# w3 times w_out as three fp32r products, w1 and w2 decoded once, landmark matrices evicted from a pair of PSUM banks

## The chip, the cores and the metric

One NeuronCore of a Trainium2 chip runs the whole program. The metric is the device time of one execution in microseconds (us). PE is the matmul engine, DVE, ACT and POOL are the vector, scalar and GpSimd engines, SP is the queue from which nearly all transfers are issued.

## The reference

Three layers follow each other, all to be computed to fp32 accuracy (fp32r is the one-pass matmul type, whose operands have fewer bits; a number is then carried as a high and a low half):

```python
# 4 batches, 8 heads, 576 tokens, 64 per head, 32 landmarks of 18 tokens
A = sm(q, k_lm); Bm = sm(q_lm, k_lm); C = sm(q_lm, k)      # scaled softmaxes
Z = Bm.transpose(0, 1, 3, 2) / (norm_1(Bm) * norm_inf(Bm) + 1e-06)
for _ in range(6):
    Z = 2 * Z - Z @ Bm @ Z
x = A @ Z @ C @ v                                          # 2304 x 512
h = (x @ w1) * (x @ w2) @ w3 @ w_out                       # w3 1024x1024, w_out 1024x512
h = h @ w_in; g = h * tanh(softplus(h)); out = g @ w_out2  # 512x2048, 2048x512
```

The weights come as float64.

## The kernel before

`ORDER` is one long string of step names, written out by hand; `issue()` walks through it and emits every step on its engine (the step's first engine, or the one behind `@`). Each engine executes its own instructions in that order. A step takes tiles from named pools (`take`) and gives them back (`free`), so the string also decides who waits for whose buffer. The last 14 of 24 output groups stand in an ordinary loop behind it.

**Weights.** A piece is 128 rows by 512 float64. `ld` (SP) loads it into a slot of `raw` (four) or `raw2` (three), `da` (ACT or DVE, line 202 or 204) turns the top 16 bits of each number into a scratch `u`, and `db` (DVE, `join`, line 214) joins the two into fp32.

**w3 times w_out.** 8 pieces `wo` and 16 pieces `w3` are decoded so; `add_w3_mm` (line 344) then makes 64 fp32 products of 128x128 by 128x512, `mm n x`, summed in eight PSUM banks, 8 products a bank. `ehi`/`elo` split a finished bank into the halves `W3[0]` and `W3[1]`.

**Attention.** `attn(b)` for the four batches: `ks`/`qs` sum the landmarks, `as` makes the scores of A and `at`, `amx`, `asb`, `aex`, `asm`, `aad`, `arc`, `amul`, `atr` its softmax by token, `ahi`/`alo` the halves in `AT`; `cs` to `cve` make C times v, `bs` to `brc` the small softmax, `nc` to `nrc` the norms, `nm`/`nu` the six iterations, `lt`/`lte` the landmark matrices `LT`. Of these only `amul` runs on POOL.

**First gate.** `m b s` (line 784) multiplies `LT` of batch b with w1 and w2 of four pieces (`w0..` for batches 0 and 1, `w1..` for 2 and 3, decoded anew from float64), into two PSUM banks; `mh`/`ml` split them into the halves `M`, 256 columns at a time. `xa`/`xb` are the products with `AT` (two times three fp32r products), `xc` and `xm` copy and multiply, `sh`/`sl` split the result, `y` multiplies it with `W3`.

**Second gate.** 24 groups of seven products (Z) and twelve output products (O), about 15.6 us each, from some 341 us on.

PSUM is one pool `w` of eight banks, given out in the order in which they come free.

Of the kernel before, what the change touches and what calls it, by code (L numbers as in the profile page):

```python
# [223 lines left out]

# [1231 lines left out]
```

## Time and profile before

| | |
|---|---|
| three runs | 718.66 us median, 717.59 to 718.89 |
| the profiled execution | 719.34 us, its span 717.5 us |
| busy share | PE 98%, DVE 58%, ACT 40%, POOL 2% |
| clock of PE, mean | 0.988 of full speed |

The page cuts the span into 40 slices of 18 us. PE is at 9 tenths or more from the third slice to the last but one; DVE is at 7 to 9 in slices two to eight and mostly at 2 to 6 behind them. A row of a timeline gives the start, the length, the engine, the line, what it writes and reads, and how many instructions it merges. An fp32 product appears as two rows (a pair of weight loads and matmuls).

### The profile page before, as it was taken

What the parts mean: (1) busy time and instruction counts of PE and PEld (TensorE: products, weight loads), DVE (VectorE), ACT (ScalarE), POOL (GpSimd) and SP (SyncE); (2) the same over time, 40 slices, a digit from 0 to 9 for tenths busy, and PEclk for the clock granted to TensorE, in tenths of its full rate; (3) what the DMA queues carried; (4) which work ended last, traced back from release to release, by engine and by line L of the source; (5) the groups of instructions that cost most, each with busy time, mean ns of one, the idle gap of its engine ahead of it and who ended that gap; (6) DMA issues with size and microseconds to landing.
All of it is one profiled execution on the core that took longest, in us unless ns stands there. A gap on an engine that the chain in (4) does not pass through costs nothing.

```text
span 717.5 us, 12433 instructions
## 1 busy us (share of the span) xinstructions
...
## 2 busy tenths in 40 slices
...
GB/s 337 318 289 242 240 206 248 108 194 148 60 89 89 90 134 219 146 207 252 315 65 220 221 350 194 291 232 248 272 211 209 163 205 206 180 219 208 171 1 88
DMA packets 33914, 141.38 MB, mean 197 GB/s; under 512 B 3392, under 2 KB 3776, under 8 KB 30272
## 3 DMA queue, kind: packets, MB, share of 16 engines
...
q8 instruction: 39, 0.64, 0.4%
...
q10 hardware_dynamic: 144, 0.13, 0.1%
HBM read 110.69 MB, written 29.88 MB: 196 GB/s over the span
## 4 chain that ended last, share of the span: by engine, by line
PE 94%; DMA 2%; DVE 2%; ACT 1%; issue 0%; SPq 0%; ACTq 0%; DVEq 0%
PE ps L194 27%; PE ps L195 27%; PE ps L196 27%; PE ps L344 7%; PE ps L784 2%; DMA raw<-in_wts_dram 2%; PE ps L405 1%; PE ps L597 1%; DMA q<-in_qT_dram 1%; PE ps L531 1%; PE ps L510 0%; DVE e L420 0%; DVE cmx L481 0%; DVE mx L426 0%; DVE ea L463 0%
## 5 line engine op out<-in xcount | busy, mean ns | idle before, releaser
L195 PE MATMUL ps<-hs,W 128*128 128x288 f32 (+1 forms) x298 | 92.3, 310 | 0.0
L194 PE MATMUL ps<-hs,W 128*128 128x288 f32 (+1 forms) x298 | 92.3, 310 | 0.0
L196 PE MATMUL ps<-hs,W 128*128 128x288 f32 (+1 forms) x298 | 92.2, 309 | 0.0
L1254 DVE TENSOR_TENSOR hsb<-ps,zt 128x384 f32<-128x384 f32 x72 | 39.7, 556 | 88.7 <-PE ps L196 88.2
L1250 ACT ACTIVATE hsb<-hsb 128x768 f32<-128x768 f32 (+1 forms) x48 | 32.8, 684 | 117.4 <-DVE hsb L1254 117.4
L194 PE MATMUL ps<-AT,M 128*128 128x288 f32 x256 | 77.4, 302 | 0.0
L196 PE MATMUL ps<-AT,M 128*128 128x288 f32 x256 | 75.5, 295 | 0.0
L195 PE MATMUL ps<-AT,M 128*128 128x288 f32 x256 | 75.4, 294 | 0.0
L1254 DVE TENSOR_TENSOR zt<-ps,zt 128x384 f32<-128x384 f32 x48 | 26.7, 556 | 83.1 <-PE ps L196 81.0
L344 PE MATMUL ps<-wo,raw 128*128 128x512 f32 x128 | 60.6, 616 | 1.3 <-DVE wo L214 1.3
L194 PEld LDWEIGHTS ps<-hs,W 128*128 128x128 f32 x298 | 56.0, 188 | 2.1 <-ACT M L218 0.8
L196 PEld LDWEIGHTS ps<-hs,W 128*128 128x128 f32 x298 | 55.9, 188 | 1.8
L195 PEld LDWEIGHTS ps<-hs,W 128*128 128x128 f32 x298 | 56.1, 188 | 1.3
L223 DVE TENSOR_TENSOR W<-hsb,W 128x384 fp32r<-128x384 f32 (+1 forms) x72 | 48.8, 686 | 9.6 <-ACT W L1251 9.5
L194 PEld LDWEIGHTS ps<-AT,M 128*128 128x128 f32 x256 | 48.0, 188 | 5.1 <-issue 2.6
L195 PEld LDWEIGHTS ps<-AT,M 128*128 128x128 f32 x256 | 48.1, 188 | 0.5 <-issue 0.5
L196 PEld LDWEIGHTS ps<-AT,M 128*128 128x128 f32 x256 | 48.0, 188 | 0.0
L344 PEld LDWEIGHTS ps<-wo,raw 128*128 128x128 f32 x128 | 24.3, 200 | 26.4 <-issue 21.1
L218 ACT ACTIVATE a<-ps 128x288 f32<-128x288 f32 x64 | 25.5, 411 | 50.9 <-PE ps L196 46.3
L202 ACT ACTIVATE top<-raw 128x512 f16<-128x512 bf16 x48 | 37.3, 785 | 8.8 <-DMA raw<-in_wts_dram 6.2
L195 PE MATMUL ps<-yH,zw 128*128 128x384 f32 x120 | 40.3, 336 | 0.1
L195 PE MATMUL ps<-yH,hs 128*128 128x384 f32 x120 | 40.2, 335 | 0.0
...
## 6 DMA issues: line engine op xcount, KB each, us to landing
...
```

The costliest lines, as they stand in the source:

```text
L194: T.matmul(out=o, lhsT=lh, rhs=rh, start=first, stop=False, skip_group_check=partial)
L195: T.matmul(out=o, lhsT=lh, rhs=rl, start=False, stop=False, skip_group_check=partial)
L196: T.matmul(out=o, lhsT=ll, rhs=rh, start=False, stop=last, skip_group_check=partial)
L202: S.activation(o, i, ACTF.Copy)
L218: S.activation(o, x, ACTF.Copy)
L223: (G if e == "POOL" else V).tensor_tensor(o, x, f32(hi), op=ALU.subtract)
L344: T.matmul(out=got(f"acc{i}"), lhsT=f32(middle(got(f"w3{n}"))[:, o:o + 128]), rhs=WO0[j // 4][:, j % 4], start=j == 0, stop=j == 7)
L405: T.matmul(out=mine(f"{key}{g}{hf}")[32 * i:32 * i + 32, 0:HALF], lhsT=st[lm][r, p, :], rhs=st[x][r, p, hf * HALF:(hf + 1) * HALF], start= ...
L531: T.matmul(out=pc[32 * i:32 * i + 32, :], lhsT=et[0:w, ck, 32 * i:32 * i + 32], rhs=VT[0:w, ck, h * D:(h + 1) * D], start=(ck == 0), stop= ...
L784: T.matmul(out=got(f"p{c}{key}")[32 * i:32 * i + 32], lhsT=LT[r, b, 2 * c + par, :], rhs=w12(f"w{bp}{s}{2 * c + par}")[r], start=True, sto ...
L1250: S.activation(e, src_, ACTF.Mish)
L1254: V.tensor_tensor(o, x, y, op=ALU.add)
```

## The change

`mm` becomes `mm3`, three fp32r products of high and low halves. So every `wo` and `w3` piece gets two more steps: `hi` (ACT or DVE) copies the decoded piece into fp32r, `lo` (POOL or DVE) subtracts it and rounds the rest; `mm` waits for `lo`. The halves of w3 lie in eight slots of `W3`, those of w_out in `WO0` and a new tile `WLO` or in two of these slots.

w1 and w2 are decoded once. `wsm` (SP) stores each decoded piece as fp32 in a DRAM tile `WMD`, and for batches 2 and 3 a plain load of 256 KB takes the place of load, `da` and `db`.

The two banks of `m` become a fixed pair, `PAIR`; one instruction splits 2 x 256 columns. Until `join` the two banks are a pool `v` for the first half of `as` of batches 0 and 1, behind `split` they go back to `w`, which has six banks until then.

In the attention `by` reads PSUM with a bias and sums as it goes, `bml` becomes two ACT instructions that sum too; `asb`, `alo` and `nml` may run on POOL, `bad`, `aad`, `nad`, `nc`, `npy` on ACT. `ORDER` is written anew. In it `bsb`, `bsm` and `ns0` are gone.

```diff
-    "ctr0 0,cev00 0,lq0 1,brc 0,cev10 0,crc0 0,at00 0,at10 0,bml 0,ns0 0,btr 0,qs3 1,ns1 0,lq1 1,qs4 1,cm11 0,"
+    "npy0 1@DVE,npy1 1@DVE,cs0 1,cs1 1,cm00 1,cm10 1,cm20 1,nm0 1,lo wo2@POOL,nu0 1,da wo3@ACT,lo w31@POOL,mm 1 0,"
...
-    pools["w"] = bank[0:8]
+    pools["w"], pools["v"], pools["m2"] = bank[0:6], bank[6:8], []
...
+    def split(u, hi, lo, take=()):
+        step(f"hi {u}", ("ACT", "DVE"), [f"db {u}"], lambda e: copy(e, hi(), f32(middle(got(u)))), take)
+        step(f"lo {u}", ("DVE", "POOL"), [f"hi {u}"], lambda e: less(e, lo(), f32(middle(got(u))), hi()), (), [u])
...
-            T.matmul(out=got(f"acc{i}"), lhsT=f32(middle(got(f"w3{n}"))[:, o:o + 128]), rhs=WO0[j // 4][:, j % 4],
-                     start=j == 0, stop=j == 7)
+            w = got(f"sw3{n}")
+            mm3(got(f"acc{i}"), W3[0][:, w, o:o + 128], W3[1][:, w, o:o + 128],
+                WO0[j // 4][:, j % 4], wo_lo(j), j == 0, j == 7)
...
-        step(me, "PE", [f"db w3{n}", f"db wo{j}"] + chain(f"mm{i}", me), mm,
-             {f"acc{i}": "w"} if j == 0 else {}, [f"w3{n}"])
+        step(me, "PE", [f"lo w3{n}", f"lo wo{j}"] + chain(f"mm{i}", me), mm,
+             {f"acc{i}": "w"} if j == 0 else {}, [f"sw3{n}"] + ([f"wol{j // 2}"] if j > 3 else []))
...
-            add(f"asb{g}", "DVE", [f"amx{g}"], a_sub(g))
+            add(f"asb{g}", ("DVE", "POOL"), [f"amx{g}"], a_sub(g))
...
-            add(f"alo{g}", "DVE", [f"ahi{g}"], a_out(g, 1), (), (), [f"ea{g}"])
+            add(f"alo{g}", ("DVE", "POOL"), [f"ahi{g}"], a_out(g, 1), (), (), [f"ea{g}"])
...
+        if bp:
+            step(f"ld {u}", "SP", [f"wsm {d}"], lambda e: nc.sync.dma_start(out=w12(u), in_=WMD[d * 128:(d + 1) * 128, :]),
+                 {"f" + u: "w12"})
+            return
...
+        step(f"wsm {d}", "SP", [f"db {u}"], lambda e: nc.sync.dma_start(out=WMD[d * 128:(d + 1) * 128, :], in_=w12(u)), (), ["f" + u])
...
-            for c in range(2):
-                step(f"mh{c} {n}", "ACT", [key, f"mt {n}"], ev(0, c, x))
-                step(f"ml{c} {n}", "DVE", [f"mh{c} {n}"], ev(1, c, x), (), [f"p{c}{key}"])
+            step(f"mh {n}", "ACT", [key] + vacated, ev(0, x), {f"M {n}": "M"})
+            step(f"ml {n}", "DVE", [f"mh {n}"], ev(1, x), (), ["p" + key])
```

On PE, the first products of w3 and w_out (line 344; `ps` is a bank, `raw` and `wo` are the decoded pieces) stand so before:

```order
L531 MATMUL ps_83<-vt,et 32x64 x20
L344 MATMUL ps_77<-wo_66,raw_73 128x512
L510 MATMUL ps_81<-idn,ce_98 128x128 x4
L512 MATMUL ps_83<-idn,ce_98 64x128
L510 MATMUL ps_84<-idn,ce_97 128x128 x4
```

And now (lines 192 to 194; `W` are the halves of w3, `wlo` is the low half of w_out):

```order
L624 MATMUL ps_78<-py 32x64 x8
L192 MATMUL ps_80<-wo_66,W_64 128x512
L193 MATMUL ps_80<-wlo,W_64 128x512
L194 MATMUL ps_80<-wo_66,W_65 128x512
L624 MATMUL ps_78<-py 32x64 x8
```

One product has become three, and the second of them reads what POOL wrote.

POOL's whole work before, behind its memsets, is eight times `amul`:

```order
L457 TENSOR_TENSOR e1_94<-e1_94,sm_402 128x576
L457 TENSOR_TENSOR e0_93<-e0_93,sm_404 128x576
L457 TENSOR_TENSOR e1_94<-e1_94,sm_596 128x576
L457 TENSOR_TENSOR e0_93<-e0_93,sm_604 128x576
L457 TENSOR_TENSOR e1_94<-e1_94,sm_1580 128x576
```

Its first instructions now (`mx`: `asb`; `cc`: `nml`; `W` and `wlo`: `lo`; `sm`: `amul`; `AT`: `alo`):

```order
L227 TENSOR_TENSOR e_92<-e_92,mx 128x576
L227 TENSOR_TENSOR cc<-nm 128x2
L227 TENSOR_TENSOR e_93<-e_93,mx 128x576
L230 TENSOR_TENSOR W_65<-raw_73,W_64 128x512
L482 TENSOR_TENSOR e_92<-e_92,sm 128x576
L230 TENSOR_TENSOR wlo<-raw_73,wo_66 128x512
L230 TENSOR_TENSOR wlo<-raw,wo_66 128x512 x2
L230 TENSOR_TENSOR W_65<-raw,W_64 128x512
L230 TENSOR_TENSOR W_65<-raw_73,W_64 128x512
L230 TENSOR_TENSOR AT_68<-ea_94,AT_68 128x576
```

Three `amul` had stood ahead of the first landmark product `m 0 0`; now 26 of POOL's 42 steps do.

PE around `m 0 0` before (`w` are the decoded pieces of w1 and w2, `cv` and `py` belong to `lt`); eight rows on, batch 1 follows on two more banks:

```order
L344 MATMUL ps_79<-wo_67,raw_73 128x512
L663 MATMUL ps_83<-py,cv 64x32 x2
L663 MATMUL ps_80<-py,cv 64x32 x2
L784 MATMUL ps_81<-w_669,LT 32x512
L784 MATMUL ps_84<-w_669,LT 32x512
```

And now (line 815; `pair` is the pair of banks):

```order
L624 MATMUL ps_78<-py 32x32 x8
L815 MATMUL pair<-w_716,LT 32x512 x8
L690 MATMUL ps_79<-py,cv 64x32 x2
L690 MATMUL ps_77<-py,cv 64x32 x2
L192 MATMUL ps_82<-wo_66,W_64 128x512
```

Batch 1's product now comes after that batch's `lt` (line 690), one product of w3 and the scores of batch 2.

## Rows read from the trace of the kernel before

**Rows 1.** Windows: length, busy us and count by engine, PE clock, DMA share, GB/s.

```profile
core 0: us, PE busy (x) PEld busy (x) DVE busy (x) ACT busy (x) POOL busy (x), PEclk, DMA share, GB/s
5.60:64.40 58.80, 50.39 (x681) 23.48 (x679) 55.64 (x140) 24.59 (x64) 5.09 (x4) 0.85 0.87 316
...
64.60:84.60 20.00, 20.00 (x140) 14.79 (x132) 18.12 (x37) 10.61 (x27) 0.00 (x0) 1.00 0.64 226
...
175.70:338.40 162.70, 162.70 (x1277) 157.20 (x1277) 100.40 (x227) 75.55 (x197) 0.00 (x0) 1.00 0.39 137
...
341.20:717.50 376.30, 371.82 (x1848) 333.49 (x1848) 171.03 (x312) 131.07 (x251) 0.00 (x0) 1.00 0.54 203
```

**Rows 2.** The chain that ended last, shares of the span by engine (the page's part 4).

```profile
PE 94%; DMA 2%; DVE 2%; ACT 1%; issue 0%; SPq 0%; ACTq 0%; DVEq 0%
```

**Rows 3.** Timeline of DVE and PE around 64 us: start, length, instruction.

```profile
63.09 1.29 DVE L214 SCALAR_TENSOR_TENSOR w<-raw,top 128x512 int32<-128x512 int32 x2
...
64.61 1.95 PE L784 MATMUL ps<-w,LT 64*32 64x512 f32 x32
```

**Rows 4.** Line 344 between 66 and 74 us: min/median/max ns, first and last start.

```profile
L344 PE MATMUL ps<-wo,raw x16: 592/592/704, 66.5 to 73.0; 128*128 128x512 f32 x16
```

**Rows 5.** Timeline of PE, the first and last of seven fp32r products of 512 columns.

```profile
625.70 0.39 PE L196 MATMUL ps<-W 128*128 128x512 f32 x1
...
627.05 0.39 PE L196 MATMUL ps<-W 128*128 128x512 f32 x1
```

**Rows 6.** Groups by line and shape, DVE: busy us, mean ns, idle before.

```profile
L223 DVE TENSOR_TENSOR M<-ps,M 128x256 fp32r<-128x256 f32 x64 | 25.1, 417 | 8.0 <-ACT M L218 6.4 <-PE ps L196 1.1
...
L214 DVE SCALAR_TENSOR_TENSOR w<-raw,top 128x512 int32<-128x512 int32 x32 | 21.7, 685 | 2.6 <-ACT top L202 2.3
L204 DVE TENSOR_SCALAR top<-raw 128x512 f16<-128x512 bf16 x40 | 18.1, 456 | 0.1
...
L431 DVE TENSOR_TENSOR e<-e,mx 128x576 f32<-128x576 f32 x8 | 6.0, 756 | 0.1
...
L223 DVE TENSOR_TENSOR W<-ps,W 128x512 fp32r<-128x512 f32 x8 | 5.4, 688 | 2.5 <-ACT W L218 2.4
```

**Rows 7.** The same view of ACT.

```profile
L202 ACT ACTIVATE top<-raw 128x512 f16<-128x512 bf16 x48 | 37.3, 785 | 8.8 <-DMA raw<-in_wts_dram 6.2 <-DVE wo L214 2.4
...
L218 ACT ACTIVATE M<-ps 128x256 fp32r<-128x256 f32 x64 | 21.5, 387 | 15.9 <-PE ps L784 10.1 <-DVE M L223 3.1 <-DVE wo L214 1.7
...
L218 ACT ACTIVATE W<-ps 128x512 fp32r<-128x512 f32 x8 | 4.8, 603 | 5.4 <-PE ps L344 5.4
...
L218 ACT ACTIVATE W<-raw 128x512 fp32r<-128x512 f32 x3 | 2.0, 667 | 2.2 <-DVE raw L214 2.2
```

**Rows 8.** Timeline of POOL, its four instructions ahead of 64 us.

```profile
37.80 1.61 POOL L457 TENSOR_TENSOR e<-e,sm 128x576 f32<-128x576 f32 x1 [36.12 <-DVE sm L452]
40.28 1.16 POOL L457 TENSOR_TENSOR e<-e,sm 128x576 f32<-128x576 f32 x1 [0.87 <-DVE sm L452]
...
49.67 1.16 POOL L457 TENSOR_TENSOR e<-e,sm 128x576 f32<-128x576 f32 x1 [8.22 <-ACT et L521]
51.30 1.16 POOL L457 TENSOR_TENSOR e<-e,sm 128x576 f32<-128x576 f32 x1 [0.48 <-DVE py L654]
```

**Rows 9.** Timeline of DVE: instructions beside those of POOL, and the same forms alone.

```profile
25.95 0.15 DVE L626 TENSOR_TENSOR cc<-nm 128x2 f32<-128x2 f32 x1
...
35.38 0.17 DVE L447 TENSOR_SCALAR sm<-sm 128x18 f32<-128x18 f32 x1
...
38.80 1.16 DVE L214 SCALAR_TENSOR_TENSOR raw<-raw,top 128x512 int32<-128x512 int32 x1
...
40.98 0.48 DVE L626 TENSOR_TENSOR cc<-nm 128x2 f32<-128x2 f32 x1
...
50.17 0.69 DVE L447 TENSOR_SCALAR sm<-sm 128x18 f32<-128x18 f32 x1
...
51.22 1.34 DVE L393 TENSOR_REDUCE sumq<-q 128x64 f32<-128x1152 f32 x1
```

More of the change, by code (lines that the diff above doesn't have):

```diff
@@ L220, in copy, with plus, pair @@
             (G if e == "POOL" else V).tensor_scalar(o, x, 1.0, 0.0, op0=ALU.mult, op1=ALU.add)
+    def plus(e, o, x, c):
+        if e == "ACT":
+            S.activation(o, x, ACTF.Copy, bias=c)
+        else:
+            V.tensor_scalar(o, x, c, None, op0=ALU.add)
+    def pair(e, o, x, y, op):
+        (G if e == "POOL" else V).tensor_tensor(o, x, y, op=op)
     def less(e, o, x, hi):
@@ L231, in kept @@
         return pe.tile(shape, dtype, tag=tag, name=name)
-    WO0 = [kept(f"Y{b}", [128, 4, 512], F32, f"wo{b}") for b in (2, 3)]
+    WO0 = [kept(f"Y{b}", [128, 4, 512], F32R, f"wo{b}") for b in (2, 3)]
     AT = {b: kept(f"Y{b}", [128, 2, 2, S_LEN], F32R, f"AT{b}") for b in (0, 1)}
@@ L249 @@
     LATE = {}
-    bank = [ps.tile([128, 512], F32, name=f"ps{i}") for i in range(8)]
+    bank = [ps.tile([128, 512], F32, name=f"ps{i}") for i in range(6)]
+    PAIR = ps.tile([128, 2, 512], F32, name="pair")
+    bank += [PAIR[:, 0], PAIR[:, 1]]
     ctx.enter_context(tc.manual_schedule())
@@ L295, in issue @@
                     free[p].append(i)
-            for key, p in moves.get(n, ()):
-                pools[p].append(got(key))
+            for _, p, x in moves.get(n, ()):
+                pools[p].append(x)
                 free[p].append(len(pools[p]) - 1)
         assert len(done) == len(steps)
-    pools["w"] = bank[0:8]
+    pools["w"], pools["v"], pools["m2"] = bank[0:6], bank[6:8], []
     pools["raw"] = [RAW[:, 1024 * i:1024 * i + 1026] for i in range(4)]
@@ L305 @@
     pools["raw2"] = [RAW2[:, 1024 * i:1024 * i + 1026] for i in range(3)]
+    pools["w3"] = list(range(8))
     pools["u"] = [TOP[:, i] for i in range(NTOP)]
@@ L309 @@
     pools["hs"] = [0, 1]
-    pools["e"], pools["ea"] = ([p0.tile([128, S_LEN], F32, name=f"{x}{i}") for i in range(2)] for x in ("e", "ea"))
+    pools["e"], pools["ea"] = ([p0.tile([128, S_LEN], F32, name=f"{x}{i}") for i in range(n)] for x, n in (("e", 2), ("ea", 1)))
+    WLO = p0.tile([128, 4, 512], F32R, name="wlo")
     pools["ce"] = [p0.tile([128, S_LEN], F32, name=f"ce{i}") for i in range(2)]
@@ L325, in raw_pool, with wo_lo @@
         return "raw2" if len(first) in RAW_M else "raw"
+    def split(u, hi, lo, take=()):
+        step(f"hi {u}", ("ACT", "DVE"), [f"db {u}"], lambda e: copy(e, hi(), f32(middle(got(u)))), take)
+        step(f"lo {u}", ("DVE", "POOL"), [f"hi {u}"], lambda e: less(e, lo(), f32(middle(got(u))), hi()), (), [u])
     def add_wo(j):
         u = f"wo{j}"
-        decode(u, j, lambda: got(u), {u: raw_pool(u)}, lambda: WO0[j // 4][:, j % 4], ((), (), [u]))
+        decode(u, j, lambda: got(u), {u: raw_pool(u)})
+        if j in (4, 6):
+            step(f"wol{j // 2}", "none", [], lambda e: None, {f"wol{j // 2}": "w3"})
+        split(u, lambda: WO0[j // 4][:, j % 4], lambda: wo_lo(j))
+        if j > 3:
+            steps[f"lo {u}"][1].append(f"wol{j // 2}")
+    def wo_lo(j):
+        return WLO[:, j] if j < 4 else W3[j % 2][:, got(f"wol{j // 2}")]
     def add_w3(n):
@@ L333, in add_w3 @@
         decode(u, 8 + n, lambda: got(u), {u: raw_pool(u)})
+        split(u, lambda: W3[0][:, got("s" + u)], lambda: W3[1][:, got("s" + u)], {"s" + u: "w3"})
         for i in range(4):
@@ L343, in mm @@
             o = a * 256 + ic * 128
-            T.matmul(out=got(f"acc{i}"), lhsT=f32(middle(got(f"w3{n}"))[:, o:o + 128]), rhs=WO0[j // 4][:, j % 4],
-                     start=j == 0, stop=j == 7)
+            w = got(f"sw3{n}")
+            mm3(got(f"acc{i}"), W3[0][:, w, o:o + 128], W3[1][:, w, o:o + 128],
+                WO0[j // 4][:, j % 4], wo_lo(j), j == 0, j == 7)
         me = f"mm {n} {x}"
-        step(me, "PE", [f"db w3{n}", f"db wo{j}"] + chain(f"mm{i}", me), mm,
-             {f"acc{i}": "w"} if j == 0 else {}, [f"w3{n}"])
+        step(me, "PE", [f"lo w3{n}", f"lo wo{j}"] + chain(f"mm{i}", me), mm,
+             {f"acc{i}": "w"} if j == 0 else {}, [f"sw3{n}"] + ([f"wol{j // 2}"] if j > 3 else []))
         if j == 7:
-            step(f"ehi {i}", "ACT", [me], lambda e: copy(e, W3[0][:, i], got(f"acc{i}")))
-            step(f"elo {i}", "DVE", [f"ehi {i}"], lambda e: less(e, W3[1][:, i], got(f"acc{i}"), W3[0][:, i]),
+            step(f"ehi {i}", "ACT", [me], lambda e: copy(e, W3[0][:, got(f"W3 {i}")], got(f"acc{i}")), {f"W3 {i}": "w3"})
+            step(f"elo {i}", "DVE", [f"ehi {i}"], lambda e: less(e, W3[1][:, got(f"W3 {i}")], got(f"acc{i}"), W3[0][:, got(f"W3 {i}")]),
                  (), [f"acc{i}"])
@@ L430, in f @@
             def f(e):
[L431 removed]
+                pair(e, by_token(g), by_token(g), st["mx", g].unsqueeze(2).to_broadcast([128, NT, L]), ALU.subtract)
             return f
@@ L446, in f @@
             def f(e):
-                V.tensor_scalar(st["sm", g], st["sm", g], 1e-9, None, op0=ALU.add)
+                plus(e, st["sm", g], st["sm", g], 1e-9)
             return f
@@ L603, in b_p0, with n_sum @@
                 tile_mm(st["pp"][:, g, :], st["bt"][:, g, :], st["bt"][:, g, :])
[L605 to L610 removed]
+        def n_sum(e):
+            V.tensor_reduce(st["ns"][:, 2:4], st["bt"], axis=AX.X, op=ALU.add)
         def n_cp(e):
             st["bc"] = sbt([128, 4, L], "bc", 1)
[L614 removed]
+            copy(e, st["bc"], st["ns"].unsqueeze(2).to_broadcast([128, 4, L]))
         def n_tr(e):
@@ L625, in n_mul @@
             st["cc"] = sbt([128, 2], "cc", 2)
-            V.tensor_tensor(st["cc"], st["nm"][:, 0:2], st["nm"][:, 2:4], op=ALU.mult)
+            pair(e, st["cc"], st["nm"][:, 0:2], st["nm"][:, 2:4], ALU.mult)
         def n_add(e):
-            V.tensor_scalar(st["cc"], st["cc"], 1e-6, None, op0=ALU.add)
+            plus(e, st["cc"], st["cc"], 1e-6)
         def n_rec(e):
@@ L637, in f @@
                     st["py"] = sbt([128, 2, 2, L], "py", 2)
-                V.tensor_tensor(st["py"][:, :, i, :], st["bm" if i else "pp"],
-                                st["cc"].unsqueeze(2).to_broadcast([128, 2, L]), op=ALU.mult)
+                x = st["bm" if i else "pp"]
+                if e == "ACT":
+                    for g in range(2):
+                        S.activation(st["py"][:, g, i, :], x[:, g, :], ACTF.Copy, scale=st["cc"][:, g:g + 1])
+                else:
+                    V.tensor_tensor(st["py"][:, :, i, :], x, st["cc"].unsqueeze(2).to_broadcast([128, 2, L]), op=ALU.mult)
             return f
@@ L686, in attn @@
         for g in range(2):
-            add(f"bmx{g}", "DVE", ["bs"], b_max(g), old(2, "bsb0", "bsb1"))
+            add(f"bmx{g}", "DVE", ["bs"], b_max(g), old(2, "bng"))
+        add("bng", "DVE", ["bmx0", "bmx1"], b_neg, old(2, "by0", "by1"))
         for g in range(2):
-            add(f"bsb{g}", "DVE", [f"bmx{g}"], b_sub(g), old(2, "bml"), (), [f"pb{g}"])
-        add("by", "ACT", ["bsb0", "bsb1"], b_exp)
-        add("bsm", "DVE", ["by"], b_sum, old(2, "bml"))
-        add("bad", "DVE", ["bsm"], b_add)
+            add(f"by{g}", "ACT", ["bng"] + ["by0"] * g, b_exp(g), old(2, "bml1"), (), [f"pb{g}"])
+        add("bad", ("DVE", "ACT"), ["by0", "by1"], b_add)
         add("brc", "DVE", ["bad"], b_rec)
-        add("bml", "DVE", ["brc"], b_mul, old(2, "npy1", "ns0"))
-        add("btr", "DVE", ["bml"], b_tr, old(2, "ns1", "bp"))
+        for g in range(2):
+            add(f"bml{g}", "ACT", ["brc"] + ["bml0"] * g, b_mul(g), old(2, "npy1", "ns1", "nc"))
+        add("btr", "DVE", ["bml0", "bml1"], b_tr, old(2, "ns1", "bp"))
         add("bp", "PE", ["btr"], b_p0, (), {"pp0": "w"})
-        add("ns0", "DVE", ["bml"], n_sum(0), old(2, "nc"))
-        add("ns1", "DVE", ["btr", "ns0"], n_sum(1))
-        add("nc", "DVE", ["ns0", "ns1"], n_cp, old(1, "ntr"))
+        add("ns1", "DVE", ["btr"], n_sum)
+        add("nc", ("DVE", "ACT"), ["bml1", "ns1"], n_cp, old(1, "ntr"))
         add("ntr", "DVE", ["nc"], n_tr, old(1, "nx"))
         add("nx", "DVE", ["ntr"], n_max, old(2, "nml"))
-        add("nml", "DVE", ["nx"], n_mul, old(2, "npy0", "npy1"))
-        add("nad", "DVE", ["nml"], n_add)
+        add("nml", ("DVE", "POOL"), ["nx"], n_mul, old(2, "npy0", "npy1"))
+        add("nad", ("DVE", "ACT"), ["nml"], n_add)
         add("nrc", "DVE", ["nad"], n_rec)
-        add("npy0", "DVE", ["bp", "nrc"], b_py(0), old(2, "lt0", "lt1"), (), ["pp0"])
-        add("npy1", "DVE", ["nrc", "bml", "npy0"], b_py(1))
+        add("npy0", ("DVE", "ACT"), ["bp", "nrc"], b_py(0), old(2, "lt0", "lt1"), (), ["pp0"])
+        add("npy1", ("DVE", "ACT"), ["nrc", "bml1", "npy0"], b_py(1))
         for k in range(6):
@@ L716, in attn @@
         for hf in range(2):
-            add(f"as{hf}", "PE", [ks, "lq1"], a_scores(hf), (), {f"sc{g}{hf}": "w" for g in range(2)})
+            add(f"as{hf}", "PE", [ks, "lq1"], a_scores(hf), (), {f"sc{g}{hf}": "w" if hf or b > 1 else "v" for g in range(2)})
         for hf in range(2):
@@ L722, in attn @@
             add(f"amx{g}", "DVE", [f"at0{g}", f"at1{g}"], a_max(g), e_old(g, "asb"))
-            add(f"asb{g}", "DVE", [f"amx{g}"], a_sub(g))
+            add(f"asb{g}", ("DVE", "POOL"), [f"amx{g}"], a_sub(g))
             add(f"aex{g}", "ACT", [f"asb{g}"], a_exp(g))
             add(f"asm{g}", "DVE", [f"aex{g}"], a_sum(g), e_old(g, "amul"))
-            add(f"aad{g}", "DVE", [f"asm{g}"], a_add(g))
+            add(f"aad{g}", ("DVE", "ACT"), [f"asm{g}"], a_add(g))
             add(f"arc{g}", "DVE", [f"aad{g}"], a_rec(g))
@@ L827, in add_ab @@
             me = f"{x} {key}"
-            step(me, "PE", [f"ml0 {b} {s}", f"ml1 {b} {s}"] + [f"alo{g} {b}" for g in range(2)] + chain("x", me), ab(i),
+            step(me, "PE", [f"ml {b} {s}"] + [f"alo{g} {b}" for g in range(2)] + chain("x", me), ab(i),
                  {"ab"[i] + key: "w"}, [f"M {b} {s}"])
@@ L1085 @@
     in_m = [first[i - 1] for i in RAW_M]
-    vacated = [f"db {u}" for u in in_m] + [f"mm {u[2:]} {i}" for u in in_m if u[1] == "3" for i in range(4)]
+    step("join", "none", [f"at0{g} 1" for g in range(2)], lambda e: None, {f"v{i}": "v" for i in range(2)})
+    moves["join"] = [("v0", "m2", PAIR)]
+    vacated = [f"lo {u}" for u in in_m]
     for s in range(NS // 2):
```

64 lines of the change are left out of this document (31 added, 33 removed), and 258 rows, old and new, of the table ORDER.

## The prediction

> **What bounds the kernel now.** I read the chain of waits first: PE holds 94% of it [rows 2]. The windows then tell two stages apart. From 5.6 us, when DVE begins, to 64.4 us DVE is busy for 55.64 of 58.80 us; PE's 50.39 are not dense work, since its clock stands at 0.85 and small products fill it [rows 1]. Behind that PE is busy for all of 20.00 us, then for all of 162.70, while DVE needs 18.12 and 100.40 [rows 1]. The seam is visible: the two decodes for the first landmark product end at 63.09 + 1.29 = 64.38 us, and `m 0 0` begins at 64.61 [rows 3]. So the start lasts as long as DVE's work ahead of `m 0 0`, and from there the end is set by the sum of PE's work. A product of w3 and w_out that PE makes ahead of `m 0 0` lies in gaps; one behind it costs its full length.
>
> **The products.** An fp32 product is two rows; 16 rows begin between 66.5 and 73.0 us, 15 steps, so 0.433 us a row and 0.867 us a product [rows 4]. fp32r products of 512 columns follow each other by (627.05 - 625.70) / 6 = 0.225 us [rows 5], so three take 0.675; with the longer steps elsewhere I take 0.68. That is 0.19 us less for each of 64, 12.0 us of PE work. But where they lie moves too. Ahead of `m 0 0` ORDER has 24 products before and 39 now; behind it 40 x 0.867 = 34.7 us become 25 x 0.68 = 17.0 us. The rest of PE's work ahead of that point is the same but for two `lt` (later) and one `bs` (earlier), about 0.2 us. PE's work behind `m 0 0` shrinks by 17.5 us.
>
> **DVE ahead of `m 0 0`.** I count the steps up to the decode that `m 0 0` waits for. More now: five `db` at 0.69, two `da` at 0.46, four `elo` and two `lo` at 0.69, three `hi` (between the 0.456 of line 204 and the 0.69 of a full copy; I take 0.6) [rows 6], two landmark sums at 1.34 [rows 9] and one `atr` at 0.75: 3.4 + 0.9 + 4.1 + 1.8 + 2.7 + 0.8 = 13.7. Fewer: four `asb` and two `alo` (0.75 each, line 431 [rows 6]), and some 18 small ones of the small softmax and the norms at 0.15 to 0.25, 8.4 in all. Net 5.3 us of durations. DVE's durations ahead of `m 0 0` sum to 63.9 us by the groups' means, but fill 55.6, since neighbours overlap; 5.3 x 55.6/63.9 = 4.6 us on the path.
>
> **POOL.** Ahead of `m 0 0` it has 26 steps instead of three (a fourth `amul` runs by 64 us). A 576-column one takes 1.16 us [rows 8], so one of 512 about 1.03; the sum is some 27 us, which fits beside 69 us. What it does to DVE doesn't fit so easily. Beside POOL's instruction of 40.28 to 41.44 us a DVE product of two columns that takes 0.15 alone takes 0.48, to 41.46; beside that of 49.67 to 50.83 an 18-column instruction of 0.17 takes 0.69, to 50.86; a `db` of 0.69 takes 1.16 beside the first [rows 8, 9]. The landmark sum of 1.34 beside the last is not touched [rows 9]. So some forms of DVE stand still until POOL is done, and POOL's own 1.61 says that it waits too. The four cost DVE 0.47, 0.33, 0.52 and 0: 1.3 us, 0.33 each. 26 of them cost 8.6, 7.3 more than before.
> The Trainium skill states it as a rule (SBUF — State Buffer, "Who interferes with whom"): DVE and GpSimd share one port pair as an exclusive lock, a DVE instruction with two SBUF inputs or in a 2-port mode contends with a GpSimd one that reads SBUF, and whoever comes second blocks fully. The rows agree (0.69 for 0.17, ending with POOL's). It speaks against moving `lo` and `asb` to POOL: each holds DVE as well as sparing it. By the rule an order that never lets the two meet pays nothing, and one that lets them meet always pays part of a POOL instruction each time; these are the first two rivals below.
>
> **The sum.** `m 0 0` comes 4.6 + 7.3 = 11.9 us later, PE behind it has 17.5 us less: 5.6 us earlier. The profiled execution took 719.34 us, span 717.5 and 1.8 around it, 0.7 over the median of 718.66; taken off the median it is **713.0 us**.
>
> **What lies beside other work.** `hi` and ACT's new steps: ACT is busy for 24.59 of 58.80 us [rows 1]; 15 `hi` at 0.667, four `ehi` at 0.603 [rows 7] and the small ones add some 20, so 45 of 69, hidden; without cover each `hi` costs 0.67 in the chain to its product. The second decode of w1 and w2: 16 `db` at 0.69 and 16 `da` (0.456 on DVE, 0.785 on ACT [rows 6, 7]) go, some 15 us of DVE, nearly all beside a PE that is dense anyway: nothing. Its transfers: 16 loads of 512 KB become 16 loads and 16 stores of 256 KB, the same bytes, at a DMA share of 0.39 [rows 1]; a `wsm` waits for its `db` on SP, and the loads queued behind it wait along. The landmark split: 64 ACT instructions of 387 ns and 64 of DVE at 417 become 32 at 603 and 32 at 688 [rows 6, 7], 5.5 and 4.7 us less, hidden. But with one pair `m` of the next batch waits for `ml` of the last: at most 2 x 0.603 + 0.688 = 1.9 us, 14 times, if ORDER put nothing between; it puts 3 to 12 us of PE work there, so I take 0. Six banks for eight: an `xa` or `xb` that finds its bank unread waits for one copy or product, at most 0.45 us; about 20 are that close now, some 14 before. 0, at most 3. Between `m 0 0` and `m 1 1` PE has 40.5 us and DVE 39.8 plus some eleven locks: 0, at most 3. The second gate keeps its instructions (371.82 of 376.30 us [rows 1]): 0, 1 either way.
>
> **Rivals.**
> *The locks cost nothing* (POOL meets only sums, transposes and PSUM reads): 11.9 becomes 4.6, and less if `hi` or the overlap are better; 12.9 us earlier, 705.8 us. For it: line 393 isn't touched [rows 9], and small additions left DVE. Against: `db`, 22 of them ahead of `m 0 0`, is a form that was held.
> *The locks decide, and the kernel becomes slower.* The place is DVE ahead of `m 0 0`: some 36 of its instructions are of held forms. If each met POOL half way or worse, at the 0.52 that was seen, it is 18.7 us: 4.6 + 18.7 - 1.3 - 17.5 = 4.5 us later, 723.2. It decides from (17.5 - 4.6 + 1.3) / 36 = 0.39 us each. For it: POOL is busy for 27 of some 50 us there, and every product waits for a `lo` behind all that POOL has queued. Against: four instructions averaged 0.33.
> *The start gives all back, without more*: locks at 0.33 and six banks, the pair and the stretch to `m 1 1` at their bounds, 3 + 3: 719.1, no change.
> *The change doesn't do what it says*: three fp32r products not faster than one fp32 one. At 0.225 against 0.433 a row, both seen on a full clock, that would take weight loads that aren't hidden; I give it no chance of its own.
>
> **How the numbers follow.** The forecast (709 to 717 us): 0.50. No locks (below 709): 0.18. All given back: 0.12. Slower: 0.20. Some 0.2% is what a measurement of this kernel can tell from no change, 1.4 us. Of the forecast's chance a little lies within it: faster 0.67, same 0.13, slower 0.20. The range leaves out a tenth on each side: from 704 (no lock and an overlap a little better) to 722 (most of the locks at their worst).
>
> **What would show it.** Products in three rows of some 0.225 us; no fp32 row of 592 ns. `m 0 0` at about 76 us (69 without locks, 87 with the worst), with 39 products made; PE dense behind it. POOL 27 us ahead of it, and DVE's `db` longer than 0.69 where POOL runs. Wrong would be: DVE idle for more than 5 us ahead of `m 0 0` (then it waits for POOL, ACT or a transfer), or gaps of PE behind it with a bank or the pair as releaser.

## The result and the profile after

The changed kernel takes 723.11 us (median of 6 runs, 721.73 to 723.44), the kernel before 718.11 (6 runs, 717.59 to 718.89): ratio 1.0066, interval 1.0054 to 1.0079. It is **slower by 5.0 us**, where the forecast was 713.0 and the range ended at 722. That is 0.7%, and no run of the one kernel lies among those of the other.

The first lines of the page of after, busy time and share by engine, and the chain of waits by engine:

```profile
PE 696.6 (97%) x5068; PEld 608.1 (84%) x5068; DVE 412.0 (57%) x817; ACT 293.6 (41%) x669; POOL 55.1 (8%) x47
...
PE 83%; DVE 5%; issue 1%; DMA 1%; ACT 1%; POOL 0%; DVEq 0%; POOLq 0%; ACTq 0%
```

PE has 83% of the chain instead of 94 [rows 2], and POOL is busy for 55 us. The windows of after, cut at its own seams (the first landmark product, the first product of the last stage), answer to [rows 1]:

```profile
core 0: us, PE busy (x) PEld busy (x) DVE busy (x) ACT busy (x) POOL busy (x), PEclk, DMA share, GB/s
5.60:78.30 72.70, 58.46 (x753) 36.54 (x751) 70.78 (x135) 41.26 (x106) 36.71 (x27) 0.86 0.80 285
78.40:98.40 20.00, 19.07 (x177) 15.05 (x178) 18.21 (x36) 9.89 (x29) 5.07 (x4) 1.00 0.90 314
78.40:339.20 260.80, 257.57 (x2431) 232.35 (x2432) 167.58 (x367) 117.55 (x305) 17.27 (x15) 1.00 0.46 158
339.20:721.50 382.30, 376.37 (x1874) 337.57 (x1872) 172.66 (x316) 133.56 (x257) 0.00 (x0) 1.00 0.54 204
```

In the start DVE is busy for all but 1.9 of 72.7 us while PE stands still for 14.2. Behind the first landmark product PE is idle for 3.2 us, where the kernel before had 0.2 (271.58 busy of 271.80). The seams in PE's timeline of after (start, length, what, idle before it), and one late wait:

```profile
78.39 1.09 PE L815 MATMUL pair<-w,LT 64*32 64x512 f32 x16 [0.33 <-DVE w L212]
...
339.24 0.34 PE L192 MATMUL ps<-yW,zw 128*128 128x384 f32 x1
...
476.95 0.50 PE L192 MATMUL pair<-wy,W 128*128 128x512 f32 x1 [1.31 <-DVE hsb L218]
```

In the kernel before the last stage begins at 336.38. So the two profiled executions compare like this:

| Stretch | before | after | forecast | measured |
|---|---|---|---|---|
| up to `m 0 0` | 64.61 | 78.39 | +11.9 | +13.8 |
| `m 0 0` to the last stage | 271.77 | 260.85 | -17.5 | -10.9 |
| the last stage | 381.12 | 382.26 | 0 | +1.1 |
| span | 717.5 | 721.5 | -5.6 | +4.0 |

The sum is 1 us short of the medians because the profiled execution of before (719.34 us) is a late one: in three kernels below that have the same start, `m 0 0` begins at 63.03, 64.00 and 63.01 us. Against those the delay up to `m 0 0` is 14.4 to 15.4 us, not 13.8.

**What POOL does to DVE.** POOL's timeline, and DVE's beside it:

```profile
24.49 1.16 POOL L482 TENSOR_TENSOR e<-e,sm 128x576 f32<-128x576 f32 x1
...
33.13 1.30 POOL L230 TENSOR_TENSOR W<-raw,W 128x512 fp32r<-128x512 f32 x1 [1.47 <-ACT W L216]
34.55 1.44 POOL L230 TENSOR_TENSOR AT<-ea,AT 128x576 fp32r<-128x576 f32 x1
...
41.26 1.31 POOL L230 TENSOR_TENSOR W<-raw,wo 128x512 fp32r<-128x512 f32 x1 [1.32 <-ACT wo L216]
42.52 1.62 POOL L482 TENSOR_TENSOR e<-e,sm 128x576 f32<-128x576 f32 x1
```

```profile
24.15 1.34 DVE L418 TENSOR_REDUCE sumq<-q 128x64 f32<-128x1152 f32 x1
...
33.25 1.21 DVE L224 TENSOR_SCALAR cc<-cc 128x2 f32<-128x2 f32 x1
...
41.56 1.56 DVE L212 SCALAR_TENSOR_TENSOR raw<-raw,top 128x512 int32<-128x512 int32 x1
...
46.52 0.68 DVE L212 SCALAR_TENSOR_TENSOR raw<-raw,top 128x512 int32<-128x512 int32 x1
...
153.79 0.17 DVE L224 TENSOR_SCALAR cc<-cc 128x2 f32<-128x2 f32 x1
```

An addition on two columns that takes 0.17 us alone (153.79) lasts 1.21 us and ends, at 34.46, with POOL's instruction of 33.13 (34.43). A decode of 0.68 (46.52) lasts 1.56 beside POOL's instruction of 41.26. The landmark sum of 1.34 beside that of 24.49 isn't touched, as in [rows 9]. Fifteen DVE instructions ahead of `m 0 0` last longer than the same forms alone while POOL works, 11.7 us together.

The first products of the first and the seventh of seven triples in a row on PE:

```profile
103.49 0.40 PE L192 MATMUL ps<-wo,W 128*128 128x512 f32 x1
...
107.67 0.40 PE L192 MATMUL ps<-wo,W 128*128 128x512 f32 x1
```

(107.67 - 103.49) / 6 = 0.70 us for a product, against 0.867 [rows 4].

### The profile page after: what moved, and what is told of

Same layout as the page of the kernel before. It is cut to its first block, busy times and chain, and to the rows that moved or that the text cites. A ratio compares the mean times of both kernels' runs of the same rounds, so it can differ in the third digit from the quotient of the medians.

```text
span 721.5 us, 12543 instructions
## 1 busy us (share of the span) xinstructions
PE 696.6 (97%) x5068; PEld 608.1 (84%) x5068; DVE 412.0 (57%) x817; ACT 293.6 (41%) x669; POOL 55.1 (8%) x47
## 4 chain that ended last, share of the span: by engine, by line
PE 83%; DVE 5%; issue 1%; DMA 1%; ACT 1%; POOL 0%; DVEq 0%; POOLq 0%; ACTq 0%
PE ps L192 23%; PE ps L194 23%; PE ps L193 23%; PE pair L192 4%; PE pair L193 4%; PE pair L194 4%; PE pair L815 2%; DMA raw<-in_wts_dram 1%; DVE W L230 1%; DVE raw L212 1%; PE ps L624 1%; DVE h L853 0%; DVE top L202 0%; DVE sumk L418 0%; DVE M L230 0%
## 5 line engine op out<-in xcount | busy, mean ns | idle before, releaser
L192 PE MATMUL ps<-hs,W 128*128 128x288 f32 (+1 forms) x252 | 77.5, 308 | 0.0
L192 PE MATMUL ps<-AT,M 128*128 128x288 f32 x252 | 76.3, 303 | 1.2 <-DVE W L230 0.6
L193 PE MATMUL ps<-hs,W 128*128 128x288 f32 (+1 forms) x252 | 77.3, 307 | 0.0
L194 PE MATMUL ps<-hs,W 128*128 128x288 f32 (+1 forms) x252 | 77.2, 306 | 0.0
L194 PE MATMUL ps<-AT,M 128*128 128x288 f32 x252 | 74.3, 295 | 0.0
L193 PE MATMUL ps<-AT,M 128*128 128x288 f32 x252 | 74.2, 295 | 0.0
L192 PEld LDWEIGHTS ps<-AT,M 128*128 128x128 f32 x252 | 47.3, 188 | 9.1 <-issue 4.2
L192 PEld LDWEIGHTS ps<-hs,W 128*128 128x128 f32 x252 | 47.4, 188 | 2.6 <-ACT y L216 0.8
L193 PEld LDWEIGHTS ps<-hs,W 128*128 128x128 f32 x252 | 47.5, 189 | 1.0
L194 PEld LDWEIGHTS ps<-hs,W 128*128 128x128 f32 x252 | 47.3, 188 | 1.2
L193 PEld LDWEIGHTS ps<-AT,M 128*128 128x128 f32 x252 | 47.3, 188 | 0.2
L194 PEld LDWEIGHTS ps<-AT,M 128*128 128x128 f32 x252 | 47.3, 188 | 0.0
L853 DVE TENSOR_TENSOR h<-a,ps 128x288 f32<-128x288 f32 x63 | 27.3, 449 | 28.2 <-PE ps L194 21.2
L1285 ACT ACTIVATE hsb<-ps 128x384 f32<-128x384 f32 x24 | 11.8, 491 | 64.9 <-PE ps L194 64.8
L212 DVE SCALAR_TENSOR_TENSOR raw<-raw,top 128x512 int32<-128x512 int32 x40 | 32.9, 821 | 8.1 <-ACT top L200 7.5
```

What stands on the lines that cost most here:

```text
L192: T.matmul(out=o, lhsT=lh, rhs=rh, start=first, stop=False, skip_group_check=partial)
L193: T.matmul(out=o, lhsT=lh, rhs=rl, start=False, stop=False, skip_group_check=partial)
L194: T.matmul(out=o, lhsT=ll, rhs=rh, start=False, stop=last, skip_group_check=partial)
L212: V.scalar_tensor_tensor(to, middle(w), 13, u, op0=ALU.logical_shift_right, op1=ALU.bitwise_or)
L853: V.tensor_tensor(hslice(u, s), got("s" + key), got("b" + key)[:, 0:HALF], op=ALU.mult)
L1285: S.activation(e, src_, ACTF.Mish)
```

## Experiments

Times are medians, ratios are against the kernel before on the same chip. That kernel took 718.0 to 718.3 us beside each of them, so differences to the changed kernel's 723.11 are good to some 0.3 us.

### e1: GpSimd's remainders left out

```diff
-  lambda e: less(e, lo(), f32(middle(got(u))), hi())
+  lambda e: less(e, lo(), f32(middle(got(u))), hi()) if e == "DVE" else None
...
-  mm3(got(f"acc{i}"), W3[0][..], W3[1][..], WO0[j // 4][:, j % 4], wo_lo(j), ..)
+  mm3(got(f"acc{i}"), W3[0][..], W3[0][..], WO0[j // 4][:, j % 4], WO0[j // 4][:, j % 4], ..)
```

> The changed kernel without the remainders that GpSimd makes: each of its lo steps issues nothing, and every product of w3 and w_out takes the rounded operands in all three of its fp32r products, so the remainders of w3 and w_out are left out of the result and TensorE's work stays what it was. In the trace of the changed kernel 16 such steps run on GpSimd ahead of the first landmark product, and nine of DVE's instructions that overlap them last some 9.0 us longer than the same forms alone. Theory (these remainders hold DVE, and DVE sets the start): the first landmark product starts at about 69.4 us instead of 78.4, and the time falls by 7 to 9 us, to 714 to 716. Rival (GpSimd only works beside, and the start is late for the extra steps on DVE alone): both stay within 1 us, 722 to 724.

712.61 us (712.13 to 713.41), ratio 0.9921 (0.9909 to 0.9934): 10.5 less than after, a little more than expected. `m 0 0` starts at 69.02. The window of its start:

```profile
5.60:68.90 63.30, 55.36 (x756) 36.44 (x754) 61.02 (x135) 41.54 (x106) 12.61 (x11) 0.89 0.90 327
```

DVE has the same 135 instructions as in the start of after and is busy for 61.02 us instead of 70.78. The 9.8 us are what 16 instructions of another engine did to it, 0.61 each. Some 2 us of holds by the other 11 are left.

### e2: the remainders on DVE

```diff
-  lo w30@POOL ... lo wo0@POOL ...   (19 of them)
+  lo w30@DVE ... lo wo0@DVE ...
```

> The changed kernel with all 19 remainders of GpSimd made by DVE, at the same places of the order. DVE gets 16 steps of 0.69 us ahead of the first landmark product, 11.0 us, and loses the 9.0 us for which it was held. Theory (a remainder on GpSimd costs DVE nearly what it spares it): the first landmark product moves by 0 to 3 us, to 78 to 81, and the time is 723 to 726. Rival (GpSimd's work is free for DVE): 11 us later, at 89, and 733 or more.

725.55 us, ratio 1.0106 (1.0092 to 1.0121), `m 0 0` at 81.95. The window of its start:

```profile
5.60:81.90 76.30, 59.28 (x753) 36.54 (x751) 71.14 (x151) 41.77 (x106) 13.80 (x11) 0.84 0.76 275
```

With 16 instructions more, DVE is busy for hardly longer than in after (71.14 us against 70.78): the time in which it now makes remainders it had lost standing still. So a remainder on POOL isn't free, and it is still a little cheaper than one on DVE: 11 us of work moved off DVE brought 2.4.

### e3: before, landmark products parted

```diff
 ORDER
-  m 0 0,m 1 0, ... mh0 0 0,mm 3 1, ...
+  m 0 0, ... mh0 0 0,mm 3 1,m 1 0, ...
```

> The kernel before with seven of its landmark products moved behind the next large product on TensorE, so that no two of them stand side by side; nothing else is changed, the sixteen landmark products leave their banks as before. In the trace of before two that stand together take 1.88 us and 0.2 of slower steps around them, 1.04 each; in the trace of after one that stands alone takes 1.02 and 0.2, 1.22. Theory (the single pair costs time because each landmark product then stands alone): 7 x 0.36 = 2.5 us more, 720 to 721. Rival (how they stand is of no account, and what is lost behind the first landmark product is lost to waits): within 0.7 us of the kernel before.

723.33 us, ratio 1.0076 (1.0063 to 1.0089), `m 0 0` at 63.03, and 276.8 us from there to the last stage instead of 271.8. How two stand in before, and one in after:

```profile
204.63 0.29 PE L196 MATMUL ps<-hs,W 128*128 128x288 f32 x1
204.85 1.95 PE L784 MATMUL ps<-w,LT 64*32 64x512 f32 x32
206.73 0.40 PE L194 MATMUL ps<-AT,M 128*128 128x288 f32 x1
206.97 0.29 PE L195 MATMUL ps<-AT,M 128*128 128x288 f32 x1
```

```profile
227.30 0.29 PE L194 MATMUL ps<-AT,M 128*128 128x288 f32 x1
227.52 1.09 PE L815 MATMUL pair<-w,LT 64*32 64x512 f32 x16
228.54 0.40 PE L192 MATMUL ps<-AT,M 128*128 128x288 f32 x1
228.77 0.29 PE L193 MATMUL ps<-AT,M 128*128 128x288 f32 x1
```

Products of 288 columns normally begin 0.13 us apart; the one ahead of a landmark product takes 0.22 (0.09 more) and the one behind 0.23 or 0.24 (0.11 more). Two side by side take 1.88 + 0.20, one alone 1.02 + 0.20: parting a pair costs 2 x 1.22 - 2.08 = 0.36 us, seven of them 2.5. PE's waits in e3 ahead of the last stage (us in total, times, longest) are the next part:

```profile
PE ps L192 <- ACT M L216: 1.1, 1, 1.1
PE ps L194 <- DVE M L221: 0.5, 1, 0.5
```

Two products wait for the eviction of a landmark product that now comes later, 1.6 us. Of the 5.0 us, 0.9 is left; 0.6 of it lies at 103 us, where products with `AT` begin up to 0.40 us apart and the profile shows no wait. The rival, no cost, is out. But the run lost twice what the theory forecast: 2.5 us are the price of standing alone, read from the rows, and the theory had missed that a landmark product made later is also evicted later.

### e4: the hold alone, in the kernel before

```diff
+  step(f"nil {u}", "POOL", [f"db {u}"], lambda e: nil(..))
+  def nil(x, y): G.tensor_tensor(NIL, x, y, op=ALU.subtract)
 ORDER
-  db wo0, ...
+  db wo0,nil wo0, ...      (15 of them)
```

> The kernel before with 15 subtractions of 128x512 added on GpSimd, one behind each decode of w_out and of w3's first seven tiles, reading that tile and writing a buffer that nobody reads; DVE and TensorE keep exactly their steps. It is the suspected cost alone. Theory (each holds DVE by as much as the remainders of the changed kernel do, 9.0 us in 16): 0.56 us each, 8 us in all, the first landmark product at 71 to 73 us, and 724 to 727. As predicted, 0.33 each: 5 us, 723. Rival (GpSimd beside DVE costs nothing): 64.6 us and 718.

729.21 us, ratio 1.0152 (1.0139 to 1.0165): 11 us, more than each theory expected. The window of the start, and `m 0 0` with the second product that stands beside it:

```profile
5.60:71.30 65.70, 49.43 (x686) 23.26 (x683) 61.63 (x140) 24.98 (x66) 19.49 (x17) 0.91 0.82 291
71.38:74.98 3.60, 3.60 (x33) 0.73 (x33) 3.56 (x8) 0.78 (x2) 1.15 (x2) 0.50 0.77 270
...
71.38 3.67 PE L790 MATMUL ps<-w,LT 64*32 64x512 f32 x32 [2.69 <-DVE w L213]
```

With the same 140 instructions as in [rows 1] DVE is busy for 61.63 us instead of 55.64: 6.0 us for the 13 subtractions of 1.04 us that have run by then (17 instructions of POOL less four `amul`), 0.46 each. DVE is idle for 0.9 us more, and so `m 0 0` comes 6.8 us later than in the profile of before. Now PE does wait for DVE's decode there, 2.69 us, and behind that standstill the pair lasts 3.60 us instead of 1.88, at a granted clock of 0.50, the lower level (1.2 GHz), where in before it is 1.00 [rows 1]. From `m 0 0` to the last stage e4 takes 274.2 us, 2.4 more than before; the pair is 1.7 of them and the eight fp32 products behind it 0.7. That is 9.2 us in the profiles, of which that of before is a late one. So the run shows the hold by itself, and its 11 us are more than the hold.

### e5 and e6: less for DVE in the start of before

```diff
-  V.tensor_scalar(st["be"][:, g, :], st["pb"][g], ..)      # subtract; then sum and product on DVE
+  S.activation(st["be"][:, g, :], st["pb"][g], ACTF.Exp, bias=.., accum_out=..)
```

```diff
 ORDER (e6, besides)
-  da wo1@DVE ... da wo5@DVE ... da w32@DVE ... da wo7@DVE
+  da wo1@ACT ... da wo5@ACT ... da w32@ACT ... da wo7@ACT
```

> The kernel before with one part of the change alone: the small softmax of each batch on ScalarE with its sums (no subtraction, sum and product of their own on DVE), and in the first two batches the additions of a constant and one copy on ScalarE too. Products, decodes, GpSimd and banks as before. Ahead of the first landmark product DVE loses, in each of two batches, two steps of 0.25, four of 0.21, two of 0.15 and two of 0.23 and gains one of 0.15: 3.9 us of durations, 3.4 on the path by 55.6/63.9. Theory (what DVE does ahead of the first landmark product sets the start, and TensorE's work the rest): that product at 61.2 us instead of 64.6, and 714 to 716. Rival (each handing over to ScalarE and back costs the chain as much as it spares DVE): 63.5 us or later, and 717 to 719.

> The last one and, besides, four of the copies of the top halves that DVE makes ahead of the first landmark product (0.456 us each) made by ScalarE (0.785), which is busy for 24.59 of 58.80 us there. Theory (DVE sets the start): 1.8 us of durations less, 1.6 on the path, the first landmark product at 59.6 us and 712 to 714. Rival (the longer copy stands in the chain from the transfer to the decode, or TensorE, busy for 50.39 of those 58.80 us, becomes the bound of the start): no gain over the last one, 714 to 716, or a loss.

718.25 us, ratio 1.0003 (0.9994 to 1.0011), and 718.21, ratio 1.0001 (0.9992 to 1.0010): no gain. `m 0 0` at 62.90 and 63.27, within the scatter of this start. DVE is busy for 52.5 and 52.2 us there instead of 55.6 [rows 1], and nothing came of it. The window of the last 20 us ahead of `m 0 0` in before, and its chain there, say why:

```profile
44.40:64.40 20.00, 19.87 (x247) 9.55 (x247) 19.67 (x42) 9.85 (x27) 2.31 (x2) 1.00 0.74 269
```

```profile
44.27 0.18 DVE py L654
44.50 0.55 PE ps L597 x32
```

PE is dense from 44.5 us on, and from there the chain runs on PE alone. In e5 this dense stretch begins at 42.83 and is as long, 20.1 us. DVE's decodes end just ahead of `m 0 0` [rows 3], but nobody waited for them: the row of 64.61 has no idle time in it. DVE has next to no slack there either, as e4 shows: less work for it gains nothing, more costs. Ahead of 44.5 us a transfer, PE and DVE take turns in the chain, and what DVE is spared it loses in waits for ACT; that this is why nothing was gained there is read from the rows, not tested. DVE's waits for ACT in the start of e5 (us in total, times, longest), 3.2 us where before there were 0.3:

```profile
DVE sm L456 <- ACT sm L222: 1.0, 2, 0.6
DVE bt L598 <- ACT bm L592: 0.9, 1, 0.9
DVE csm L502 <- ACT ce L495: 0.5, 1, 0.5
...
DVE cc L634 <- ACT cc L222: 0.4, 1, 0.4
...
DVE wo L212 <- ACT top L200: 0.4, 1, 0.4
```

### e7 and e8: the third batch behind `m 0 0`

```diff
 ORDER (after)
-  lk0 2,ks3 2,lq0 2,qs3 2, ... cs0 2,cs1 2,cm00 2, ... m 0 0
+  m 0 0, ... lk0 2,ks3 2, ... mm 15 2, ... cs0 2,cs1 2,cm00 2, ...
```

> The changed kernel in another order only: what it does for the third batch ahead of the first landmark product (loads of k and q, four landmark sums of 1.34 us on DVE, two score products on TensorE, and on DVE four maxima of 0.44 and two of 0.2) comes behind it, and the fourth batch's steps follow later too. The same 39 products of w3 and w_out stand ahead. DVE has 7.6 us of durations less there, TensorE 1.4. Theory (in the changed kernel DVE sets the start, TensorE waits 14 of its 73 us, and behind it TensorE has no idle time to give): the first landmark product 6 to 7.5 us earlier, at 71 to 72.5, TensorE's work behind it 1.4 longer, 717 to 719 in all. Rival (what is moved comes back, since DVE is in the chain of waits up to 118 us): the first landmark product moves, the time stays at 721 to 723. Second rival (the transfers set the start, at 285 GB/s): neither moves.

> The last one without the remainders that GpSimd makes (left out of the result, as in the first experiment: the rounded operands stand in all three products). Theory (holds of DVE by GpSimd add to what DVE does there): again 8 to 10 us less, the first landmark product at 62 to 64 us, 707 to 710 in all. Rival (with less for DVE to do, GpSimd meets it less, or TensorE, which has some 58 us of work there, is the bound by then): less than 5 us between the two.

756.53 us, ratio 1.0529 (1.0512 to 1.0546), and 747.66, ratio 1.0406 (1.0390 to 1.0422). No theory had this. `m 0 0` came at 75.65, only 2.7 us earlier, and behind it PE waited. PE's longest waits between 72 and 230 us in e7 (us in total, times, longest):

```profile
PE ps L621 <- DVE py L678: 10.3, 5, 4.7
PE ps L687 <- DVE py L678: 3.2, 1, 3.2
```

These are the steps of a batch's serial chain of small products. In this order the scores of the third batch stand among the last products of w3, the fourth batch's steps follow later still, and both chains run with little beside them to fill PE. That the order is the cause is read from it, not tested. The pair of runs doesn't tell what DVE's 7.6 us in the start are worth. It does repeat e1 in another order: without the remainders 8.9 us less.

### e9 and e11: triples behind the start only, in the kernel before

```diff
+  if n in (8, 12):
+      mm3(got(f"acc{i}"), w3_part(n, 0)[..], w3_part(n, 1)[..], wo_part(j, 0), wo_part(j, 1), ..)
 ORDER
+  xb 0 1 0,oh 0,ol 0 ... xb 0 1 1,oh 1,ol 1 ... db w38,hi w38,lo w38 ... db w312,hi w312,lo w312
 ORDER (e11, instead)
+  xb 0 2 1,oh 0,ol 0 ... xb 1 2 1,oh 1,ol 1 ... xc 0 7 0,hi w38 ... xm 0 7 0,lo w38
```

> The kernel before with eight of its 64 products of w3 and w_out as three fp32r products, those of two tiles of w3 that are made some 80 us behind the first landmark product, where TensorE is never idle; their four halves of w_out and w3 are split there by ScalarE and DVE, GpSimd gets nothing, the start stays as it was. Theory (the triple is worth what the rows say where it lies behind the start: 0.867 - 0.69 us each): 8 x 0.18 = 1.4 us less, 716.5 to 717. Rival (the splits, four of 0.667 us on ScalarE and four of 0.69 on DVE, or the products' later operands give it back): 718 to 719.

> The last kernel but one (eight products as triples, all behind the first landmark product) in another order: the two splits of w_out stand some 10 us later, where DVE is busy for 13.7 of 18.0 us in the kernel before instead of 18.1 of 20.0, the split of w3 behind the copy that a landmark product's partner waits for, and its four products behind that. In the trace of that kernel TensorE stood still for 0.86 us at 86.88 us until DVE was done and for 0.41 us at 132.18 until ScalarE was done, both where a split had been put in; its triples did cost 0.70 us. Theory (the gain was there and was given back in these two waits): 1.1 to 1.4 us less than the kernel before, 716.8 to 717.1. Rival (splits behind the first landmark product cost TensorE time wherever they stand): 718 to 719.

e9: 719.01 us, ratio 1.0014 (1.0005 to 1.0023), slower by a hair, as the rival had it. PE's waits in e9 behind the start:

```profile
86.88 0.65 PE L574 MATMUL ps<-sumk,sumq 64*32 64x32 f32 x16 [0.86 <-DVE h L842]
...
132.18 0.40 PE L192 MATMUL ps<-AT,M 128*128 128x288 f32 x1 [0.41 <-ACT a L216]
```

Neither wait is in before. Two splits, put at the end of a stretch where DVE is busy for 18 of 20 us [rows 1], cost PE 0.86 us, and one on ACT 0.41. e11, the same kernel with its splits elsewhere: 717.32 us, ratio 0.9990 (0.9981 to 0.9999), 0.7 us less than before and, each against its own before, 1.5 less than e9. That is half of what was expected: by the starts of the rows its products took 1.1 us less, and a wait of 0.42 for ACT is left at 131.84. It is the only kernel here with the whole computation that is faster than both, by no more than eight products can give.

### e10: the large softmax back on DVE

```diff
 ORDER (after)
-  asb0 0@POOL ... alo0 0@POOL ...   (14 of them)
+  asb0 0@DVE ... alo0 0@DVE ...
```

> The changed kernel with the large softmax's subtractions and its remainders back on DVE, as before the change (14 steps, six of them ahead of the first landmark product); the remainders of w3 and w_out stay on GpSimd. DVE gets four steps of 0.756 us and two of 0.744 ahead of that product, 4.5 us, and loses the part of the 2.7 us for which it was held by other steps than those of w3 and w_out. Theory (a step on GpSimd costs DVE most of what it spares it): the first landmark product 2 to 3 us later, 724 to 726. Rival (these steps on GpSimd hold DVE for longer than they last on it): 720 to 722.

730.49 us, ratio 1.0172 (1.0158 to 1.0186), `m 0 0` at 84.56: 7.4 us more than after, where 1 to 3 were expected. The window of its start:

```profile
5.60:84.50 78.90, 63.14 (x753) 40.32 (x751) 72.71 (x141) 41.26 (x106) 26.92 (x20) 0.76 0.76 270
```

DVE is busy for only 1.9 us more than in after, since it is held less, but it is idle for 6.2 us instead of 1.9, of which it waits 3.7 for ACT and 1.1 for PE; after has no such waits in its start. Two causes lie side by side here: in this order DVE's new steps make others late, and PE's mean clock is 0.76 instead of 0.86, with the same 753 instructions taking 63.14 us of busy time instead of 58.46. The run doesn't separate them. In this order these steps are better placed on POOL, and it is the remainders of w3 and w_out that cost (e1). What an edit costs in an order planned without it can be more than its own time.

## Why the prediction was wrong

**The products: right, a little small.** Products behind `m 0 0` took 34.4 us before and 17.7 now, by the distances of their starts; 16.7 less where 17.7 was forecast (0.70 a triple, not 0.68).

**The additions on DVE: right in size.** Without the holds the first landmark product was to come at 69 us; in e1, with the remainders gone and 11 other steps left on POOL, it comes at 69.02. That it fits so closely is luck, since some 2 us of holds are left in e1 and the profile of before is a late one. And the argument under it was not right. *"So the start lasts as long as DVE's work ahead of `m 0 0`"* read two rows that follow each other as a release. In the kernel before PE is dense from 44.5 us on, less work for DVE doesn't bring `m 0 0` earlier (e5, e6), and a product there doesn't lie in gaps. The sum survived because in after DVE is the bound: it is idle for 1.9 us of its start, PE for 14.2.

**POOL's holds: right mechanism, the largest miss in size ahead of `m 0 0`.** The step *"The four cost DVE 0.47, 0.33, 0.52 and 0: 1.3 us, 0.33 each. 26 of them cost 8.6"* took a mean over four cases (`ORDER` of before has four `amul` ahead of `m 0 0`, not three). Held instructions sum to 11.7 us in after, and at an equal count of instructions DVE is busier by 0.46 for a subtraction (e4) and by 0.61 for a remainder (e1). One reason is in the rows of POOL: a remainder takes 1.30 us where I took 1.03, and up to 1.75 where POOL itself waits, so POOL was busy for 36.7 us, not 27. Leaving the remainders out is worth 10.5 us (e1) and turns the loss of 5.0 into a gain of 5.6.
Beside POOL the decode of 41.56, which reads two tiles, lasts 1.56 us instead of 0.68, and the landmark sum of 24.15 its usual 1.34. The Trainium skill's rule that I cited (SBUF — State Buffer, "Who interferes with whom") is borne out by both: it has instructions with two inputs in SBUF contend with GpSimd, and `tensor_reduce` never.

**What was taken at nothing: the step that turned the sign.** *"I take 0"* for the pair, *"0, at most 3"* for six banks, *"0, at most 3"* for the stretch behind `m 0 0` and *"0, 1 either way"* for the second gate. All four went to the bad side, 6.4 us together, more than the 5.6 that were to be gained. The pair came out dear in another way than I had bounded it: not by waiting for its eviction but because each landmark product now stands alone. Before, seven pairs of them stood side by side; that is 7 x 0.36 = 2.5 us, and by the starts of all rows the landmark products and the large ones beside them did take 2.6 us longer in after. PE's waits between `m 0 0` and the last stage in after (us in total, times, longest):

```profile
PE ps L624 <- issue: 0.9, 1, 0.9
PE ps L192 <- DVE W L230: 0.6, 1, 0.6
PE ps L192 <- DVE h L853: 0.6, 1, 0.6
PE pair L192 <- ACT y L216: 0.5, 1, 0.5
PE ps L430 <- ACT LT L216: 0.3, 1, 0.3
```

2.9 us, 0.2 in before: 1.2 for DVE, 0.5 for a bank of the pair, 0.3 for `LT`, 0.9 with no releaser that the profile shows. By their releasers the 1.2 us are waits of products with `AT` for a bank that DVE is still reading; whether two more banks would have spared them no run tests. The small products that now come later are 0.5, where 0.2 was forecast. -16.7 + 2.6 + 2.7 + 0.5 = -10.9, as measured. Gaps of PE behind `m 0 0` with a bank or the pair as releaser were among the prediction's own signs of being wrong. The wait of 1.31 us at 476.95 for a bank of the pair is the last stage's +1.1; it comes back in e1 and e2 (382.3 us each) and in no kernel made from before (381.2).

**The rivals.** The time is that of *"the locks decide"*, 723.2, but not its sum: it priced the holds at 18.7 us, and they cost 10 to 12. Of the 9.6 us between forecast and measurement in the profiles, some 2 lie ahead of `m 0 0`, 6.6 behind it and 1.1 in the last stage. That costs on the same side could add up was in *"the start gives all back"* with 719, and in no rival together with a dearer hold.

**Still open:** 0.9 us of e3, the 0.9 us without a releaser, what PE's clock does to e10, and what a better order of the changed kernel could give (e7 was no answer).
